# T5-bias attention followed by a leaky-ReLU feed-forward: the second feed-forward product as seven half-block products per 512-token tile, x in a ring of four batches, and a new order table

## The chip, the cores and the metric

The kernel runs on one core of one Trainium2 chip. The metric is device time in microseconds (us) of one execution, from outside the program; below it is given as the median of three executions. The profile is of one execution, and its span runs from the first to the last instruction of the core. The engines of the core are named as the profile names them: PE (matrix multiply; PEld is its loading of the stationary operand), DVE (vector), ACT (scalar and activation), POOL (here: memsets and the issue of loads) and SP (issue of transposing DMAs and of stores).

## What is computed

Eight batches of eight heads of attention (576 tokens, head size 64) with a relative-position bias, and then two products with a leaky ReLU between them, over all 4608 tokens:

```python
scores = scale * np.matmul(q, k.transpose(0, 1, 3, 2))          # 8, 8, 576, 576
bias = bias_table[bucket]
scores = scores + bias.transpose(2, 0, 1)[None, :, :, :]
attn = softmax(scores)
attn_out = np.matmul(attn, v)                                    # 8, 8, 576, 64
x = attn_out.transpose(0, 2, 1, 3).reshape(4608, 512)
h = x @ w_in                                                     # w_in 512 x 2048
g = np.maximum(0.01 * h, h)
out = g @ w_out                                                  # w_out 2048 x 512
```

Inputs and output are float32; the products run on bf16 operands with float32 sums.

## The kernel before

**Attention.** The work goes by items, one per batch and pair of heads: 32 items, `n = 4 * b + p`. For each item six units of scores go to PSUM (`score`, L424 to L432), ACT takes the exponential of each into the bf16 tile `at` (`expo`, L438, L440, L445), DVE multiplies the band near the diagonal by the exponentiated bias (`band`, L458), PE multiplies with v (`av` and `av_tail`, L478, L493), and DVE divides by the row sums into `opair` (`norm`, L505 and L506). `opair` is turned into `xT`, tokens along the free axis, in most items by a transposing DMA that SP issues (`x_dma`, L512), in the others by PE and a copy (`x_pe`, `x_copy`). q and k come in by POOL's loads, are copied into `pr` (L368), turned (by DMA into `tu`, or by PE) and copied into `qt` and `kt` (L399).

**Feed-forward.** The 4608 tokens are nine tiles of 512, `T = 0..8`. In a tile, the first product makes 16 blocks of 128 features: for each `f`, four matmuls of 512 columns into a PSUM bank (`ffn_in`, L536) and a leaky ReLU by ACT into the bf16 tile `gt` (`ffn_act`, L540). The second product takes the tile's four groups of 128 tokens one after the other: 16 matmuls of 512 columns each into one PSUM bank, with a block of `gt` as stationary operand and a block of `w_out_sb` as moving operand (`ffn_out`, L561), then a DVE copy into `y` (`ffn_y`, L566) and a 256 KB store by SP (`ffn_store`, L571). The last group of the last tile is cut by columns into 256, 128 and 128 (`ffn_end`, L547), each with a copy and a store of its own, so that little is left behind the last matmul. `gt` has two buffers, `y` four.

**PSUM** is eight banks: two double banks for scores (`S`), one bank for one head's attention output (`O`), and three banks (`M`) that everything else shares: the other head's output, the transposes and both feed-forward products.

**The order.** All engines run a program in a fixed order. The class `Plan` lists the work as tasks with costs, predecessors and PSUM slots and lays them out greedily; its tables `SHIFT`, `HOLD` and `SWAP` move single tasks in rank, hold them to a time or put them on another engine. What comes out is one order per engine, and each engine waits at an instruction until what that instruction needs is there. The feed-forward tasks fill PE between the attention steps, about 28 matmuls of 512 columns per item; what is left of them runs after the last item. The items are also paced by the first product (`PACE`, `LEAD` in `plan_pair`).

`w_out` is loaded as two halves by POOL (`load_w_out`, L342), behind the loads of the second batch. `xT` holds all 4608 tokens.

Of the kernel before, what the change touches and what calls it, by code (L numbers as in the profile page):

```python
# [36 lines left out]
class Plan:  # L37
# [5 lines left out]
        45: 10.5, 85: 76.5, 114: -31.5, 182: -25.5, 190: 10068.5, 237: -223, 253: 17.5, 327: 9898.5, 910:  # L43
        -9994.5, 916: -10001.5, 918: -9977.5, 920: -9885.5, 922: -9978.5, 928: -7, 940: -10006.5, 942: -22, 974:
        -10001.5, 978: -24.5,
# [7 lines left out]
    }  # L53

    SWAP = (19, 88, 91, 120, 184, 212,)
# [99 lines left out]
def kernel(  # L155
# [17 lines left out]
    P = 128  # L173
# [9 lines left out]
    BAND = 128  # L183

# [4 lines left out]
    pr_pool = ctx.enter_context(tc.tile_pool(name="pr", bufs=4))  # L189
    tu_pool = ctx.enter_context(tc.tile_pool(name="tu", bufs=4))  # L190
# [3 lines left out]
    y_pool = ctx.enter_context(tc.tile_pool(name="y", bufs=4))  # L194
# [65 lines left out]
    junk = per.tile([P, 512], BF16, name="junk")  # L260
# [248 lines left out]
    def x_dma(n):  # L509
        b, p = items[n]  # L510
        w = (NJ + 1) * P
        nc.sync.dma_start_transpose(  # L512
            out=xT[p][:, b * S : b * S + w].rearrange("p (i t) -> p i t", t=P),
            in_=opairs[n].rearrange("p i d -> p (i d)"),
        )
# [6 lines left out]
    def x_copy(n, t, lo=0, hi=S):  # L522
        b, p = items[n]
        mover(t)(out=xT[p][:, b * S + lo : b * S + hi], in_=outs.pop((n, "x", lo // P))[:, lo:hi])
# [4 lines left out]
    def ffn_in(T, f, cs=range(n_cc)):  # L529
        t0, w = tiles[T]  # L530
        if cs[0] == 0:
            if T not in gts:
                gts[T] = gt_pool.tile([P, n_fc, TT], BF16, name="gt", tag="gt")
            pms[T, f] = ps_m_pool.tile([P, TT], FP32, name="pm1", tag="m")
        for c in cs:
            nc.tensor.matmul(pms[T, f], lhsT=w_in_sb[:, c, f * P : (f + 1) * P], rhs=xT[c][:, t0 : t0 + w],  # L536
                             start=(c == 0), stop=(c == n_cc - 1))
# [4 lines left out]
    def ffn_end(T, ts, lo, hi):  # L542
        if lo == 0:
            ys[T, ts] = y_pool.tile([P, DM], FP32, name="y")
        ps = outs["end", lo] = ps_m_pool.tile([P, hi - lo], FP32, name="pm2", tag="m")
        for f in range(n_fc):
            nc.tensor.matmul(ps, lhsT=gts[T][:, f, ts * P : (ts + 1) * P], rhs=w_out_sb[:, f, lo:hi],  # L547
                             start=(f == 0), stop=(f == n_fc - 1))

    def ffn_end_y(T, ts, lo, hi, copy):  # L550
        copy(out=ys[T, ts][:, lo:hi], in_=outs["end", lo])

    def ffn_end_store(T, ts, lo, hi, eng):
        t0 = tiles[T][0] + ts * P
        eng.dma_start(out=out[t0 : t0 + P, lo:hi], in_=ys[T, ts][:, lo:hi])

    def ffn_out(T, ts, i):
        if i == 0:
            ys[T, ts] = ps_m_pool.tile([P, DM], FP32, name="pm2", tag="m")
        for f in range(4 * i, 4 * i + 4):  # L560
# [288 lines left out]
```

## Time and profile before

| | |
|---|---|
| time, median of three executions | 375.85 us (375.51 to 376.46) |
| span of the profiled execution | 373.5 us |
| median time less that span | 2.35 us |
| instructions in the profile | 8628 |
| granted PE clock | 1.000 |
| ACT, first product's leaky ReLU (L540) | 144 instructions, 605 ns each |
| POOL busy | 69.4 us (19% of the span) |
| bytes read and written | 36.70 MB and 9.44 MB |

An execution's own time is its span and what lies around it, before the first and after the last instruction of the core; the page gives the span, and the 2.35 us is the difference to the median of the three timed runs, all of which lie within 0.95 us of each other. A matmul's duration in the profile is longer than the time to the next matmul, since they are pipelined; the pace of a row of matmuls is found from its first start to its last start. The same holds, by less, for DVE.

### The profile page before, as it was taken

The numbers are of one execution on the slowest core, as the hardware profiler recorded it, in microseconds if no ns is written. First come the engines' busy times: TensorE is split into PE (matmuls) and PEld (weight loads), VectorE is DVE, ScalarE is ACT, GpSimd is POOL, SyncE is SP. The second block draws the span as 40 slices with busy tenths as digits, with TensorE's granted clock in tenths as the row PEclk, the third lists the DMA queues.
The fourth block names the chain that finished last, engine by engine and source line by source line (L and its number), as shares of the span: only waits on it lengthen the run. The fifth ranks groups of instructions, "written<-read, shape, count | busy, mean of one in ns | idle before, by whom it ended". The sixth has DMA issues, their size and how long they took to land.

```text
span 373.5 us, 8628 instructions
## 1 busy us (share of the span) xinstructions
PE 368.0 (99%) x3556; PEld 191.7 (51%) x3556; DVE 204.0 (55%) x550; ACT 243.7 (65%) x351; POOL 69.4 (19%) x107
## 2 busy tenths in 40 slices
PE   8999999999999999999999999999999999999996
PEld 5675555545555555545555555545555544444444
DVE  7997567786786557655755676555643311001021
ACT  5998987588756995697667866977678333333300
POOL 8856023340025003500350013000000000000000
PEclk9999999999999999999999999999999999999999
DMA  8999999999469907991899159201210101001012
GB/s 121 156 181 197 185 181 114 212 212 176 64 132 183 177 18 111 189 157 20 131 198 146 30 113 137 71 11 47 75 47 20 47 28 54 32 28 58 28 56 86
DMA packets 103735, 39.51 MB, mean 106 GB/s; under 512 B 83472, under 2 KB 98192, under 8 KB 103696
## 3 DMA queue, kind: packets, MB, share of 16 engines
q0 software_dynamic: 53424, 18.21, 46.2%
q1 hardware_dynamic: 49920, 20.39, 29.1%
q8 instruction: 28, 0.46, 0.5%
q10 hardware_dynamic: 352, 0.36, 0.3%
q14 instruction: 11, 0.09, 0.1%
HBM read 36.70 MB, written 9.44 MB: 124 GB/s over the span
## 4 chain that ended last, share of the span: by engine, by line
PE 95%; ACT 3%; DVE 1%; issue 1%; POOL 0%; POOLq 0%
PE pm L536 34%; PE pm L561 33%; PE ps_s L424 9%; PE ps_om L493 6%; PE ps_o L493 5%; ACT at L438 2%; PE ps_s L428 2%; PE ps_s L431 2%; PE pm L547 1%; PE ps_o L478 1%; PE ps_tx L520 1%; PE ps_t L382 0%; DVE hots L301 0%; PE ps_t L387 0%; PE ps_w L814 0%
## 5 line engine op out<-in xcount | busy, mean ns | idle before, releaser
L438 ACT ACTIVATE at<-ps_s 128x1024 bf16<-128x1024 f32 x124 | 120.4, 1028 | 32.8 <-PE ps_s L424 32.8
L536 PE MATMUL pm<-xT,w_in_sb 128*128 128x512 bf16 x576 | 140.8, 379 | 0.0
L561 PE MATMUL pm<-w_out_sb,gt 128*128 128x512 bf16 x560 | 135.5, 379 | 0.0
L540 ACT ACTIVATE gt<-pm 128x512 bf16<-128x512 f32 x144 | 84.8, 605 | 59.8 <-PE pm L536 58.8
L458 DVE TENSOR_TENSOR at<-at,hk 128x768 bf16<-128x768 bf16 (+4 forms) x156 | 69.5, 453 | 64.0 <-ACT at L438 47.1
L561 PEld LDWEIGHTS <-gt 128*128 128x128 bf16 x560 | 52.5, 98 | 64.7 <-issue 5.1
L536 PEld LDWEIGHTS <-w_in_sb 128*128 128x128 bf16 x576 | 52.2, 98 | 63.1 <-issue 6.4
L566 DVE COPY y<-pm 128x512 f32<-128x512 f32 x35 | 24.2, 691 | 70.6 <-PE pm L561 70.6
L236 POOL DMA_DIRECT2D vn<-in_v_dram x32 | 28.9, 911 | 141.3 <-PE ps_o L493 131.0
L493 PEld LDWEIGHTS <-at 128*128 128x128 bf16 x1240 | 41.2, 98 | 3.7 <-issue 0.7
L424 PE MATMUL ps_s<-qt,kt 64*128 64x512 bf16 x256 | 40.0, 381 | 0.3
L440 ACT ACTIVATE at<-ps_s 128x512 bf16<-128x512 f32 x31 | 18.7, 602 | 16.7 <-PE ps_s L428 16.6
L493 PE MATMUL ps_o<-vn,at 128*128 128x65 bf16 x640 | 25.5, 193 | 0.0
L493 PE MATMUL ps_om<-vn,at 128*128 128x65 bf16 x600 | 24.1, 195 | 0.0
L424 PEld LDWEIGHTS <-kt 64*128 64x128 bf16 x256 | 8.3, 94 | 24.7 <-issue 22.0
L445 ACT ACTIVATE at<-ps_s 128x576 bf16<-128x576 f32 x31 | 20.3, 654 | 0.8 <-PE ps_s L432 0.7
L506 DVE TENSOR_TENSOR opair<-ps_o,rcp 128x320 bf16<-128x320 f32 (+2 forms) x34 | 16.4, 482 | 1.2
L506 DVE TENSOR_TENSOR opair<-ps_om,rcp 128x320 bf16<-128x320 f32 (+2 forms) x32 | 15.4, 481 | 1.1
L399 DVE COPY kt<-tu 128x576 bf16<-128x576 bf16 x24 | 15.9, 663 | 0.0
L399 DVE COPY qt<-tu 128x576 bf16<-128x576 bf16 x23 | 15.0, 652 | 0.0
L505 DVE RECIPROCAL rcp<-ps_om 128x5 f32<-128x5 f32 (+2 forms) x32 | 6.1, 192 | 15.3 <-PE ps_om L493 15.3
L228 POOL DMA_DIRECT2D kn<-in_k_dram x17 | 12.1, 715 | 9.0 <-DMA w_in_sb<-in_moe_w_in_dram 3.9
(86 smaller groups left out, 238.3 us busy)
## 6 DMA issues: line engine op xcount, KB each, us to landing
out_dram<-y SPq DMA_DIRECT2D x35, 256.0 KB, 2.0
vn<-in_v_dram POOLq DMA_DIRECT2D x32, 128.0 KB, 6.9
qn<-in_q_dram POOLq DMA_DIRECT2D x14, 288.0 KB, 10.4
kn<-in_k_dram POOLq DMA_DIRECT2D x14, 288.0 KB, 10.8
w_in_sb<-in_moe_w_in_dram POOLq DMA_DIRECT2D x2, 1024.0 KB, 11.5
w_out_sb<-in_moe_w_out_dram POOLq DMA_DIRECT2D x2, 1024.0 KB, 19.6
qn<-in_q_dram POOLq DMA_DIRECT2D x4, 144.0 KB, 4.0
v<-in_v_dram POOLq DMA_DIRECT2D x16, 32.0 KB, 7.4
```

Source lines behind the costliest of these rows:

```text
L236: nc.gpsimd.dma_start(out=vn[i][:, c, :, 0:D], in_=v[b, :, c * P : (c + 1) * P, :].rearrange("h s d -> s h d"),)
L399: copy(out=t[:, 0:S].rearrange("p (r c) -> p r c", c=NC), in_=src)
L424: nc.tensor.matmul(ps[:, e, :], lhsT=kt[r, u * P : (u + 1) * P], rhs=qt[r, 0:512], start=True, stop=True)
L438: nc.scalar.activation(at[:, :, u, 0:512], ps, AF.Exp, scale=scale)
L445: nc.scalar.activation(at4[:, 0:S], ps.rearrange("p e i -> p (e i)")[:, 0:S], AF.Exp, scale=scale)
L458: nc.vector.tensor_tensor(out=o, in0=o, in1=m, op=ALU.mult)
L493: nc.tensor.matmul(ps[:, ic, :], lhsT=at[:, o : o + P], rhs=vn[i][:, c, 2 * p + e, :], start=whole and c == 0, stop=not whole and ic == NJ ...
L506: nc.vector.tensor_tensor(out=opairs[n][:, lo:hi, e * D : (e + 1) * D], in0=ps[:, lo:hi, 0:D], in1=rcp.to_broadcast([P, hi - lo, D]), op=A ...
L536: nc.tensor.matmul(pms[T, f], lhsT=w_in_sb[:, c, f * P : (f + 1) * P], rhs=xT[c][:, t0 : t0 + w], start=(c == 0), stop=(c == n_cc - 1))
L540: nc.scalar.activation(gts[T][:, f, :], pms.pop((T, f)), AF.Prelu, bias=0.0, scale=1.0, alpha=0.01)
L561: nc.tensor.matmul(ys[T, ts], lhsT=gts[T][:, f, ts * P : (ts + 1) * P], rhs=w_out_sb[:, f, :], start=(f == 0), stop=(f == n_fc - 1))
L566: nc.vector.tensor_copy(out=y, in_=ys[T, ts])
```

## The change

The second product of a tile is computed by Strassen's scheme in Winograd's form. `g` of the tile (512 tokens by 2048 features) is seen as two by two blocks: tokens 0 to 255 and 256 to 511, features in alternate groups of 128. `w_out` (2048 by 512) is seen as two by two blocks: the same alternate groups of 128 rows, and columns 0 to 255 and 256 to 511. Seven products of half-blocks replace eight.

- **PE.** Each product is two groups of 128 tokens by eight blocks of 128 features, that is 16 matmuls of 256 columns into one bank (`product`, L604 of the new kernel): 112 matmuls of 256 columns per tile in place of 64 of 512.
- **DVE, sums of g.** Four combinations of the blocks of `gt` (`mix_g`, L582), in two halves of the features: eight instructions of 128 x 1024 bf16 per tile. Three go to new single tiles `sums`, one is written over a block of `gt`.
- **DVE, sums of w_out.** Four combinations, once, in two halves (`mix_weights`, L568 to L571): eight instructions of 128 x 1024 bf16, behind the load of each half of `w_out`. One is written over a block of `w_out_sb`.
- **DVE, output.** In place of four copies of 128 x 512 per tile, each product is taken out of PSUM by one instruction that adds it to `y` (`combine`, L612 and L617): one copy and five sums of 512 elements, and one sum of 1024 for the product that two blocks share. Two of the nine copies go to ACT by `SWAP`.
- **Stores.** `y` is one buffer for a tile, and its two halves of 256 tokens are stored by two DMAs of 512 KB (`ffn_store`, L621). The cut of the last group is gone.
- **x.** `xT` holds four batches (2304 tokens) as a ring. A write of x of batch 4 or later waits for the first product of the tile that last reads what it overwrites (`free_x`). The tile that lies across the end of the ring (T = 4) runs each of its matmuls of the first product as two of 256 columns.
- **Buffers.** `pr` and `tu` have three buffers, not four.
- **Order.** `SHIFT`, `HOLD` and `SWAP` are new.

```diff
     SHIFT = {
-        45: 10.5, 85: 76.5, 114: -31.5, 182: -25.5, 190: 10068.5, 237: -223, 253: 17.5, 327: 9898.5, 910:
...
+        36: 486.5, 43: 362.5, 60: 11.5, 66: -54.5, 68: -313, 81: 1183.5, 119: -494.5, 126: -591.5, 150: 46, 176:
...
-    SWAP = (19, 88, 91, 120, 184, 212,)
+    SWAP = (62, 63, 88, 91, 117, 184, 212, 261, 269, 270, 952, 1141,)
...
+    NPR, NTU = 3, 3
...
-    xT = [per.tile([P, NT + P - SL], BF16, name=f"xT{p}") for p in range(n_pairs)]
+    RING = 4
+    RT = RING * S
+    xT = [per.tile([P, RT + P - SL], BF16, name=f"xT{p}") for p in range(n_pairs)]
...
+    NK = n_fc // 2
+    HT, HE = TT // 2, DM // 2
+    y = per.tile([P, 2, 2, 2, HE], FP32, name="y")
+    mix = per.tile([P, 3, NK, HE], BF16, name="mix")
+    sums = [per.tile([P, NK, HT], BF16, name=f"sum{i}") for i in range(3)]
...
+            for i, (o, x, n) in enumerate(spans):
+                nc.tensor.matmul(pms[T, f][:, o : o + n], lhsT=w_in_sb[:, c, f * P : (f + 1) * P], rhs=xT[c][:, x : x + n],
+                                 start=(c == 0 and i == 0), stop=(c == n_cc - 1 and i == len(spans) - 1))
...
-    def ffn_out(T, ts, i):
...
-        for f in range(4 * i, 4 * i + 4):
-            nc.tensor.matmul(ys[T, ts], lhsT=gts[T][:, f, ts * P : (ts + 1) * P], rhs=w_out_sb[:, f, :],
-                             start=(f == 0), stop=(f == n_fc - 1))
...
+    def mix_weights(lo, hi):
+
+        (b11, b12), (b21, b22) = [[w_blocks[:, lo:hi, h, g, :] for g in range(2)] for h in range(2)]
+        m2, m3, m4 = [mix[:, i, lo:hi, :] for i in range(3)]
+        nc.vector.tensor_tensor(out=m3, in0=b22, in1=b12, op=ALU.subtract)
+        nc.vector.tensor_tensor(out=b12, in0=b12, in1=b11, op=ALU.subtract)
+        nc.vector.tensor_tensor(out=m2, in0=b22, in1=b12, op=ALU.subtract)
+        nc.vector.tensor_tensor(out=m4, in0=b21, in1=m2, op=ALU.subtract)
...
+    def mix_g(T, k, lo, hi):
+
+        a11, a12, a21, a22 = [g_block(T, r, h, lo, hi) for r in range(2) for h in range(2)]
+        s1, s2, s4 = [t[:, lo:hi, :] for t in sums]
+        out_, x, y, op = ((s1, a21, a22, ALU.add), (s2, s1, a11, ALU.subtract),
+                         (a21, a11, a21, ALU.subtract), (s4, a12, s2, ALU.subtract))[k]
+        nc.vector.tensor_tensor(out=out_, in0=x, in1=y, op=op)
...
+    def product(T, k, ts):
+
+        if ts == 0:
+            pms[T, "p", k] = ps_m_pool.tile([P, 2, HE], FP32, name="pm2", tag="m")
+        ps = pms[T, "p", k]
+        of = factors(T, k)
+        for j in range(NK):
+            l, r = of(j)
+            nc.tensor.matmul(ps[:, ts, :], lhsT=l[:, ts * P : (ts + 1) * P], rhs=r,
+                             start=ts == 0 and j == 0, stop=ts == 1 and j == NK - 1)
+
+    def combine(T, k, copy=None):
+
+        c11, c12, c21, c22 = [y[:, r, :, g, :] for r in range(2) for g in range(2)]
+        ps = pms.pop((T, "p", k))
+        if k == 1:
+            copy(out=c22, in_=ps)
+            return
+        out_, x = {2: (c11, c22), 6: (c12, c22), 7: (c22, c12), 4: (c21, c22), 5: (y[:, :, :, 1, :],) * 2, 3: (c12, c12)}[k]
+        if k == 5:
+            ps = ps.unsqueeze(1).to_broadcast([P, 2, 2, HE])
+        nc.vector.tensor_tensor(out=out_, in0=ps, in1=x, op=ALU.add)
+
+    def ffn_store(T, r):
+        t0 = tiles[T][0] + r * HT
+        nc.sync.dma_start(out=out[t0 : t0 + HT, :].rearrange("(s p) e -> p s e", p=P),
+                          in_=y[:, r].rearrange("p s g e -> p s (g e)"))
...
+        free_x = [("in", ((b - RING + 1) * S - 1) // TT, n_fc - 1)] if b >= RING else []
...
+    ORDER = (1, 2, 6, 7, 4, 5, 3)
```

Where the order moved, at two places.

**The first tile's sums, DVE.** Before, at the place where the first output group of tile 0 is copied out of PSUM (`y<-pm`), DVE stands so (`at` bands, `kt`, `qt` and `pr` copies, `xT` copy):

```order
L458 TENSOR_TENSOR at_114<-at_114,hk 128x2x384
L399 COPY kt_110<-tu 128x576
L524 COPY xT_94<-ps_tx 128x576
L403 TENSOR_TENSOR kt_110<-kt_110,own 128x128
L403 TENSOR_TENSOR qt<-qt,own 128x128
L458 TENSOR_TENSOR at_114<-at_114,hk 128x2x320
L458 TENSOR_TENSOR at_1_116<-at_1_116,hk_100 128x192
L368 COPY pr<-qn_101 96x768
L368 COPY pr<-kn_103 96x768
L458 TENSOR_TENSOR at_113<-at_113,hk 128x2x256
L566 COPY y<-pm_1166 128x512
L458 TENSOR_TENSOR at_113<-at_113,hk 128x2x384
```

Now the second half of the sums of `w_out` (L568 to L571) and the second half of tile 0's sums of g (L582) stand between the bands of one item:

```order
L471 TENSOR_TENSOR at_116<-at_116,hk 128x2x384
L568 TENSOR_TENSOR mix<-w_out_sb 128x1024
L569 TENSOR_TENSOR w_out_sb<-w_out_sb 128x4x256
L570 TENSOR_TENSOR mix<-w_out_sb 128x1024
L571 TENSOR_TENSOR mix<-w_out_sb,mix 128x1024
L582 TENSOR_TENSOR sum_98<-gt 128x1024
L538 COPY xT_91<-ps_tx 128x576
L471 TENSOR_TENSOR at_1_118<-at_1_118,hk_102 128x192
L381 COPY pr<-qn_103 96x768
L381 COPY pr<-kn_105 96x768
```

Two rows of `pr` copies like the last two follow there, and then the item's last band (`at_116`, 128x2x320). The first band of that item stands ahead of the quoted rows, and between it and the last band DVE now has the four sums of `w_out` and one of g.

**The end, DVE and SP.** Before, the last rows of DVE are copies alone (the last group's two pieces are L551), and the last of SP are stores:

```order
L566 COPY y<-pm_5348 128x512
L566 COPY y<-pm_5368 128x512
L566 COPY y<-pm_5388 128x512
L551 COPY y<-pm_5409 128x256
L551 COPY y<-pm_5429 128x128
```

```order
L512 DMA_TRANSPOSE xT_94<-opair 128x5x128
L512 DMA_TRANSPOSE xT_95<-opair 128x5x128
L571 DMA out_dram<-y 128x512 x13
L555 DMA out_dram<-y 128x256
L555 DMA out_dram<-y 128x128
```

Now the last tile's sums of g stand between the sums into `y` (`pm_5830` and `pm_5854` are the last two products of tile 7, the five numbers above 5870 that stand here are tile 8's):

```order
L617 TENSOR_TENSOR y<-pm_5830,y 128x4x256
L582 TENSOR_TENSOR sum_98<-gt 128x1024 x2
L582 TENSOR_TENSOR sum_99<-sum_98,gt 128x1024
L617 TENSOR_TENSOR y<-pm_5854,y 128x2x256
...
L612 COPY y<-pm_5875 128x2x256
...
L617 TENSOR_TENSOR y<-pm_5896,y 128x2x256
...
L617 TENSOR_TENSOR y<-pm_5954,y 128x2x256
L617 TENSOR_TENSOR y<-pm_5972,y 128x4x256
L617 TENSOR_TENSOR y<-pm_5990,y 128x2x256
```

```order
L525 DMA_TRANSPOSE xT_93<-opair 128x5x128
L525 DMA_TRANSPOSE xT_90<-opair 128x5x128
L621 DMA out_dram<-y 128x2x512
L525 DMA_TRANSPOSE xT_91<-opair 128x5x128
L525 DMA_TRANSPOSE xT_92<-opair 128x5x128
L621 DMA out_dram<-y 128x2x512 x7
```

Behind the last matmul there now stands a sum of 512 elements and a store of 512 KB, where there stood ACT's copy of 128 elements and a store of 64 KB.

More of the change, by code (lines that the diff above doesn't have):

```diff
@@ L259 @@
     make_identity(nc, ident)
-    junk = per.tile([P, 512], BF16, name="junk")
+    junk = per.tile([P, 256], BF16, name="junk")
     nc.vector.memset(junk, 0.0)
@@ new lines, in plan_ffn @@
+        cb, last = {}, []
+        for n, k in enumerate(ORDER):
+            ps = prod[T, k] = []
+            for ts in range(2):
+                rank = 10000 + (T + 1) * 64 + (2 * n + ts) * 64 / 14 + 2
+                ps.append(add("PE", 0.876, acts + mixed + of.get(k, []) + last,
+                              lambda k=k, ts=ts: product(T, k, ts), rank, take=["M"] if ts == 0 else []))
+                last = ps[-1:]
+            before = [cb[i] for i in {1: (), 2: (1,), 6: (1,), 7: (6, 2), 4: (7,), 5: (7, 4), 3: (5,)}[k]]
+            if k == 2:
+                before = before + stored.get(T - 1, [])[1:]
+            if k == 1:
+                before = before + stored.get(T - 1, [])[:1]
+            cb[k] = add("DVE", 1.2 if k == 5 else 0.66, ps + before, lambda k=k: combine(T, k, mover(cb[1])), 0, give=["M"])
+            if k == 1:
+                cb[k]["other"] = ("ACT", 0.53)
+            if k == 5:
+                stored[T] = [add("SP", 0.1, [cb[5], cb[4]], lambda: ffn_store(T, 1), 10000, tail=2.5)]
@@ L806 @@
         plan_pair(n)
+    mixed = [add("DVE", 2.4, [L["w_out", h]], lambda h=h: mix_weights(h * NK // 2, (h + 1) * NK // 2), 10000)
+             for h in range(2)]
     for T in range(n_tt):
```

94 lines of the change are left out of this document (40 added, 54 removed), and 15 rows, old and new, of tables (HOLD, SHIFT).

## The prediction

> **What bounds the kernel now.** I read the page first: shares of the engines, the slices, and the chain of work that ended last.
>
> ```profile
> span 373.5 us, 8628 instructions
> PE 368.0 (99%) x3556; PEld 191.7 (51%) x3556; DVE 204.0 (55%) x550; ACT 243.7 (65%) x351; POOL 69.4 (19%) x107
> PEclk9999999999999999999999999999999999999999
> PE 95%; ACT 3%; DVE 1%; issue 1%; POOL 0%; POOLq 0%
> PE pm L536 34%; PE pm L561 33%; PE ps_s L424 9%; PE ps_om L493 6%; PE ps_o L493 5%; ACT at L438 2%; PE ps_s L428 2%; PE ps_s L431 2%; PE pm L547 1%; PE ps_o L478 1%; PE ps_tx L520 1%; PE ps_t L382 0%; DVE hots L301 0%; PE ps_t L387 0%; PE ps_w L814 0%
> ```
>
> PE is busy for 99% of the span at full clock and makes 95% of the chain; the second product (L561) alone is a third of it. A busy PE need not be at its peak, so I looked at the pace of matmuls that follow each other in the timeline, with the mean durations from the groups of instructions by shape.
>
> ```profile
> 361.75 5.34 PE L561 MATMUL pm<-w_out_sb,gt 128*128 128x512 bf16 x24
> 366.93 1.25 PE L547 MATMUL pm<-w_out_sb,gt 128*128 128x256 bf16 x10
> 366.93 3.70 PE L547 MATMUL pm<-w_out_sb,gt 128*128 128x256 bf16 x48
> L561 PE MATMUL pm<-w_out_sb,gt 128*128 128x512 bf16 x560 | 135.5, 379 | 0.0
> L547 PE MATMUL pm<-w_out_sb,gt 128*128 128x256 bf16 x16 | 1.9, 272 | 0.0
> ```
>
> In the first, second and third row the columns are start, length from first start to last end, and count. Start to start, 512 columns take (5.34 - 0.379) / 23 = 0.2157 us, and 256 columns (1.25 - 0.272) / 9 = 0.109 us, almost exactly half. The third row is the whole last token group of today: 3.70 us. So PE's time is proportional to columns at this size, and PE really is the bound: columns removed are time removed, wherever PE keeps finding its operands ready.
>
> **The products, on the path.** A tile takes 64 x 0.2157 = 13.80 us before and 112 x 0.109 = 12.21 us after: 1.59 us less. Eight tiles give 12.7 us. The ninth takes 48 x 0.2157 + 3.70 = 14.05 us before, so 1.84 us less. Sum **-14.5 us**. The tile across the ring's end runs 128 matmuls of 256 in place of 64 of 512 in its first product: 128 x 0.109 - 64 x 0.2157 = **+0.15 us**. The rest of PE's work is unchanged in kind and count, but for two more warming matmuls at the start.
>
> The weight loads beside these matmuls double in density. They are a row of their own:
>
> ```profile
> L561 PEld LDWEIGHTS <-gt 128*128 128x128 bf16 x560 | 52.5, 98 | 64.7 <-issue 5.1
> 108.04 0.79 PE L493 MATMUL ps_om<-vn,at 128*128 128x65 bf16 x20
> ```
>
> A load lasts 98 ns, under the 109 ns of a 256-column matmul, and in the second row twenty matmuls of 65 columns, each with a load, start within 0.79 us, so at most 0.04 us apart. Loads do not set the pace at 256 columns; I count nothing for them.
>
> [...]
>
> **The end, on the path.** Today a small copy by ACT and a small store follow the last matmul.
>
> ```profile
> 370.66 0.27 ACT L551 COPY y<-pm 128x128 f32<-128x128 f32 x1 [14.16 <-PE pm L547]
> 370.96 0.38 ACTq L555 DMA_DIRECT2D out_dram<-y  x1
> out_dram<-y SPq DMA_DIRECT2D x35, 256.0 KB, 2.0
> out_dram<-y ACTq DMA_DIRECT2D x1, 64.0 KB, 1.7
> L566 DVE COPY y<-pm 128x512 f32<-128x512 f32 x35 | 24.2, 691 | 70.6 <-PE pm L561 70.6
> ```
>
> The last matmul ends at 366.93 + 3.70 = 370.63 and the span at 373.5: 2.87 us. After the change a 512-element sum (0.69 us as the copy in the last row, 0.42 more than the 0.27) and a 512 KB store follow. Its landing isn't in the trace: 1.7 us as for 64 KB is the least, and doubling the 2.0 us of the 256 KB store is the most, 4.0. From 64 to 256 KB cost 0.3 us, so I take 2.8, nearer the 2.0: 1.1 more. Sum **+1.5 us**, bounds +0.4 to +2.7.
>
> **DVE, which now has to keep up.** The new instructions' forms aren't in the trace, so I take them from the nearest rows.
>
> ```profile
> L458 DVE TENSOR_TENSOR at<-at,hk 128x768 bf16<-128x768 bf16 x62 | 34.0, 553 | 12.6 <-ACT at L438 12.4
> L458 DVE TENSOR_TENSOR at<-at,hk 128x512 bf16<-128x512 bf16 x32 | 13.5, 423 | 34.7 <-ACT at L438 34.7
> L506 DVE TENSOR_TENSOR opair<-ps_o,rcp 128x320 bf16<-128x320 f32 x32 | 15.7, 492 | 1.1
> 40.00:280.00 240.00, 240.00 (x2427) 123.02 (x2425) 154.06 (x409) 178.09 (x250) 42.15 (x55) 1.00 0.91 120
> 60.00:80.00 20.00, 20.00 (x217) 10.46 (x216) 16.71 (x42) 11.95 (x16) 9.29 (x13) 1.00 1.47 175
> ```
>
> Two bf16 operands in SBUF cost (553 - 423) / 256 = 0.51 ns per element, so a sum of 1024 takes 0.68 us. With float32 from PSUM it is (691 - 492) / 192 = 1.04 ns, so 1024 elements take 1.22 us and 512 take 0.69. A tile gets 8 x 0.68 + 6 x 0.69 + 1.22 = 10.8 us, less the four copies of 2.8: **8.1 us more DVE per tile**, and 8 x 0.68 = 5.5 us once for `w_out`. The last two rows are busy time by stage (after the window's length PE, PEld, DVE, ACT, POOL): in the 240 us where attention and feed-forward are mixed, DVE was busy 154 us, 64%. By the order, about six tiles' second products lie there: 154 + 6 x 8.1 + 5.5 = 208 us, 87%. The fullest 20 us of before had 16.71, 84%, with PE busy throughout. So on average PE covers DVE, with little to spare; ACT's work is the same but for two copies.
>
> What counts then are lumps. In the timeline the same place of two successive items starts so:
>
> ```profile
> 104.65 2.76 PE L561 MATMUL pm<-w_out_sb,gt 128*128 128x512 bf16 x12
> 113.83 0.39 PE L561 MATMUL pm<-w_out_sb,gt 128*128 128x512 bf16 x1
> ```
>
> An item is 9.18 us. The thickest lump is tile 0: eight sums of `w_out` and eight of g, 16 x 0.68 = 10.9 us, within about two items, so DVE's 64% of 18.4, 11.8 us, becomes 22.7: 4.3 too much. Behind these sums in DVE's order stand the item's last band, which `av` waits for, and the normalization, on which x hangs. PE has about half an item, 4.6 us, of other work between a score and its `av`; that absorbs most. The wait for `w_out` in DVE's queue is the other thing there:
>
> ```profile
> L342 POOL DMA_DIRECT2D w_out_sb<-in_moe_w_out_dram x2: 876/884/891, 29.0 to 30.8; - x2
> DMA to landing us min/median/max: 17.3/19.6/22.0
> ```
>
> The second half lands by 30.8 + 22.0 = 52.8 us, and DVE comes to it about an item after the first half's sums, near 54; what is later is paid by the bands behind it. Bounds of this lump: 0, if the cover holds, to 4.3 + 1; I take **+1.5**. Later tiles bring eight sums and no `w_out`: 5.4 us in the same two items, so 11.8 + 5.4 + 3.8 for combines, 21.0 against 18.4 at the worst, and idle DVE time around them (the L566 row above: 70.6 us of waiting for L561 alone). Bounds 0 to 2.6 for each of five; I take **+0.5** in all, near the lower end since the sums need only be done before the third product of a tile, 3.5 us of PE after the first begins.
>
> At the end, tile 8's sums (5.4 us) stand among tile 7's and 8's combines (5.4 us per tile): 10.8 us in the 12.2 us of a tile's products; sums of g wait until tile 7's last products have read the old ones. The first product that needs them is the third, 3 x 1.74 us after product 5 of tile 7 plus 0.86 for the last matmuls of L536: 6.1 us, and they take 1.2 + 4 x 0.68 + 0.69 = 4.6. I count nothing; without that cover it is 1 to 2 us.
>
> Counted at nothing as well: three buffers for `pr` and `tu` (a turning DMA has two items, 18 us, of lead), the ring's waits (x of batch 7 needs the first product of tile 4, which stands some four items earlier in the order), and stores, now 18 in place of 38 and one buffer, which the last tile's first combine needs back 4.4 us after tile 7's product 5, some 4.0 us after which the store lands (1.2 for the sum, 2.8).
>
> **Sum.** -14.5 + 0.15 + 1.5 + 1.5 + 0.5 = -10.85. On the profiled execution: 373.5 - 10.85 = 362.65 us of span, with the 2.35 us between span and median 365.0 us. The profile agrees with the timed runs as far as their 0.95 us of spread goes.
>
> **The rivals.**
>
> *DVE sets the pace of the mixed stage.* If the 84% of its fullest window are all that its in-order queue can be filled, 208 us need 248: 8 us more than the 240, in place of the 2.0 above, so **371 us**. For it: the bands wait for ACT and now stand behind sums. Against: PE was fully busy at 84%.
>
> *Slower: the sums run at one element per cycle.* If `gt` cut into strided blocks costs the 1.04 ns per element of the PSUM rows, a sum takes 1.22 us, and the 56 of the mixed stage need 30 us more: 238 of 240. At a fill of 90% that stage lasts 264 us: 24 more, **387 us**. It decides from about 1.0 us per sum on. Against: the bands, also cut in runs and one operand reversed, take 0.51 ns.
>
> *PE doesn't gain.* If 256-column matmuls run at 0.1232 us or more (13.80 / 112) when operands change between `gt`, sums and mixes, nothing is gained and end and lumps are paid: **379 us**. Ten in a row at 0.109 speak against it.
>
> *More is gained.* Lumps hidden, store as quick as one of 256 KB, and an order that waits 2 us less in the first 30 us: 375.85 - 14.35 + 0.7 - 2 = **360 us**.
>
> **How the numbers follow.** Forecast, 361.5 to 368: 0.68. Better: 0.08. DVE's pace, 368 to 374.7: 0.14. Gain eaten up by it exactly, within 0.3% (what a measurement of this kernel can tell from no change): 0.03. Slower: 0.05 by slow sums, 0.02 by PE's pace. So faster 0.90, same 0.03, slower 0.07. The range for 8 in 10 is 360.5 to 371.5: it takes in half of the better and half of DVE's case.
>
> **What would show it.** Products: 1008 matmuls of 256 columns, ten of them in about 1.25 us, and some 110 us in the second product in place of 124. DVE: sums near 0.68 us, the big combine near 1.22, DVE busy near 280 us in all. Lumps: PE's idle time or stretched runs between 45 and 70 us, released by DVE. End: some 4.4 us from the last matmul to the end of the span. The forecast is wrong if sums take over 1 us, if the mixed stage lasts longer than before with DVE ahead of PE in the waits, or if PE's pace at 256 columns isn't half of that at 512.

## The result, and the profile after

| | before | after |
|---|---|---|
| time, median of 11 executions (lowest to highest) | 376.46 us (375.51 to 376.99) | 370.59 us (368.09 to 374.37) |
| ratio after/before, 95% interval | | 0.9833 (0.9803 to 0.9863) |
| profiled execution, its own time | | 368.75 us |
| its span, mean granted PE clock | 373.5 us, 1.000 | 367.0 us, 0.998 |

The ratio leaves out the executions most disturbed by a low clock. The gain is 5.9 us at the median where 11 were forecast; and the kernel, steady within 1.5 us before, now varies by 6. Its executions have mean granted clocks from 0.999 (368.1 us) to 0.989 (373.0 to 374.4 us).

The page of the changed kernel, the rows that answer to those of before:

```profile
span 367.0 us, 9617 instructions
PE 355.8 (97%) x4022; PEld 239.7 (65%) x4022; DVE 266.8 (73%) x650; ACT 246.5 (67%) x356; POOL 71.8 (20%) x107
PE 87%; DVE 5%; ACT 3%; DMA 3%; issue 1%; ACTq 0%
PE pm L556 32%; PE pm L604 28%; PE ps_s L437 8%; PE ps_om L506 5%; PE ps_o L506 5%; DMA tu<-pr 3%; ACT at L451 2%; PE ps_s L441 2%; PE ps_s L444 2%; PE ps_w L879 2%; DVE at L471 1%; PE ps_o L491 1%; DVE sum L582 1%; PE ps_tx L533 1%; DVE opair L519 0%
```

PE is still the bound, but its share of the span fell from 99% to 97%. In the chain DVE grew from 1% to 5%, and 3% DMA are new, all of one kind, the DMA that turns `pr` into `tu`. The new instructions' durations, from the groups by shape (busy us, mean ns of one, idle before):

```profile
L582 DVE TENSOR_TENSOR sum<-gt 128x1024 bf16<-128x1024 bf16 x18 | 12.3, 688 | 11.1 <-ACT gt L560 11.0
L617 DVE TENSOR_TENSOR y<-pm,y 128x512 f32<-128x512 f32 x45 | 30.9, 686 | 12.8 <-PE pm L604 11.3 <-DMA out_dram<-y 1.1
L617 DVE TENSOR_TENSOR y<-pm,y 128x1024 f32<-128x1024 f32 x9 | 11.0, 1223 | 8.0 <-PE pm L604 8.0
```

0.69, 0.69 and 1.22 us, as estimated from the nearest rows of before. The last of the chain's longest rows gives the pace of the products:

```profile
348.11 13.99 PE pm L604 x128
```

13.99 / 128 = 0.109 us per 256-column matmul. The product's price was right. What was not right stands between 40 and 80 us. PE's busy time there is the number behind the window's length; the first row is of before, the other two of after:

```profile
40.00:60.00 20.00, 20.00 (x211) 10.64 (x209) 12.14 (x33) 17.51 (x25) 4.54 (x7) 1.00 1.70 171
40.00:60.00 20.00, 18.92 (x211) 10.87 (x211) 17.99 (x41) 18.39 (x27) 5.45 (x8) 1.00 1.72 176
60.00:80.00 20.00, 17.52 (x234) 13.15 (x233) 15.66 (x41) 11.19 (x16) 5.25 (x5) 1.00 1.04 118
```

Before the change both windows had 20.00 (the row from 60 to 80 us stands in the prediction). PE's waits between 40 and 100 us (us in total, times, longest), where before has none at all:

```profile
PE ps_om L491 <- DVE y L617: 1.7, 1, 1.7
PE ps_om L506 <- DVE at L471: 0.8, 1, 0.8
PE ps_s L437 <- ACT at L453: 0.7, 1, 0.7
PE ps_s L437 <- ACT at L451: 0.2, 1, 0.2
```

The two longest are one event. The chain from 66 to 74 us shows it from its cause on (start, length, what):

```profile
60.68 9.75 DMA tu<-pr
...
70.46 0.62 DVE pr L381 x2
71.08 0.57 DVE at L471 x2
71.66 0.60 DVE y L617
```

and DVE's timeline shows what waited:

```profile
70.46 0.36 DVE L381 COPY pr<-qn 96x768 bf16<-96x768 bf16 x1 [4.20 <-DMA tu<-pr]
```

DVE stood idle for 4.20 us at a `pr` copy, that of item 11. With three `pr` buffers it takes the one that item 9 used, and item 9's turning DMA, issued at 60.68 us, landed 9.75 us later. Before the change item 9's DMA took 8.3 us, not much less, but with four buffers no `pr` copy waited for it. Nobody needed item 11's copy yet: what is made of it is copied out of `tu` at 86.32 us. But behind it in DVE's order stood two bands, a sum into `y` and then more bands. The sum frees the PSUM bank that the next `av_tail` opens, the bands are `av`'s operand:

```profile
70.41 0.19 PE L491 MATMUL ps_o<-v,at 64*128 64x65 bf16 x1
72.31 0.19 PE L491 MATMUL ps_om<-v,at 64*128 64x65 bf16 x1 [1.71 <-DVE y L617]
...
73.38 0.79 PE L506 MATMUL ps_om<-vn,at 128*128 128x65 bf16 x20 [0.76 <-DVE at L471]
```

From start to start PE loses 72.31 - 70.41 = 1.90 us, and 0.95 more ahead of the last row: **2.85 us**. At the end of the span:

```profile
360.83 1.26 PE L604 MATMUL pm<-w_out_sb,sum 128*128 128x256 bf16 x10
361.62 1.59 SPq L621 DMA_DIRECT2D out_dram<-y  x2
362.12 0.69 DVE L617 TENSOR_TENSOR y<-pm,y 128x512 f32<-128x512 f32 x1 [0.52 <-PE pm L604]
```

and the landing of the last two stores, from the DMA view (count, KB each, median us):

```profile
out_dram<-y SPq DMA_DIRECT2D x2, 512.0 KB, 2.9
```

The last matmul ends at 360.83 + 1.26 = 362.09 us, the span at 367.0: 4.9 us, where 4.4 was forecast.

### The profile page after: what moved, and what is told of

Its sections match the earlier page's. It is cut to its first block, busy times and chain, and to the rows that moved or that the text cites. A ratio compares the mean times of both kernels' runs of the same rounds, so it can differ in the third digit from the quotient of the medians.

```text
span 367.0 us, 9617 instructions
## 1 busy us (share of the span) xinstructions
PE 355.8 (97%) x4022; PEld 239.7 (65%) x4022; DVE 266.8 (73%) x650; ACT 246.5 (67%) x356; POOL 71.8 (20%) x107
## 4 chain that ended last, share of the span: by engine, by line
PE 87%; DVE 5%; ACT 3%; DMA 3%; issue 1%; ACTq 0%
PE pm L556 32%; PE pm L604 28%; PE ps_s L437 8%; PE ps_om L506 5%; PE ps_o L506 5%; DMA tu<-pr 3%; ACT at L451 2%; PE ps_s L441 2%; PE ps_s L444 2%; PE ps_w L879 2%; DVE at L471 1%; PE ps_o L491 1%; DVE sum L582 1%; PE ps_tx L533 1%; DVE opair L519 0%
## 5 line engine op out<-in xcount | busy, mean ns | idle before, releaser
L556 PE MATMUL pm<-xT,w_in_sb 128*128 128x512 bf16 (+1 forms) x640 | 134.1, 358 | 0.0
L556 PEld LDWEIGHTS <-w_in_sb 128*128 128x128 bf16 x640 | 59.1, 98 | 57.1 <-issue 5.1
L471 DVE TENSOR_TENSOR at<-at,hk 128x768 bf16<-128x768 bf16 (+4 forms) x156 | 67.1, 448 | 30.6 <-ACT at L451 22.6
L604 PEld LDWEIGHTS <-gt 128*128 128x128 bf16 x576 | 54.6, 98 | 10.8 <-issue 3.6
L617 DVE TENSOR_TENSOR y<-pm,y 128x512 f32<-128x512 f32 (+1 forms) x54 | 41.9, 775 | 20.8 <-PE pm L604 19.3
L604 PEld LDWEIGHTS <-sum 128*128 128x128 bf16 x432 | 41.3, 98 | 9.6 <-issue 2.5
L604 PE MATMUL pm<-w_out_sb,sum 128*128 128x256 bf16 x288 | 35.4, 273 | 0.0
L604 PE MATMUL pm<-mix,gt 128*128 128x256 bf16 x288 | 34.8, 273 | 0.0
L604 PE MATMUL pm<-w_out_sb,gt 128*128 128x256 bf16 x288 | 33.9, 273 | 0.0
L582 DVE TENSOR_TENSOR sum<-gt 128x1024 bf16<-128x1024 bf16 x18 | 12.3, 688 | 11.1 <-ACT gt L560 11.0
L604 PE MATMUL pm<-mix,sum 128*128 128x256 bf16 x144 | 17.7, 273 | 0.0
```

What stands on the lines that cost most here:

```text
L471: nc.vector.tensor_tensor(out=o, in0=o, in1=m, op=ALU.mult)
L556: nc.tensor.matmul(pms[T, f][:, o : o + n], lhsT=w_in_sb[:, c, f * P : (f + 1) * P], rhs=xT[c][:, x : x + n], start=(c == 0 and i == 0), s ...
L604: nc.tensor.matmul(ps[:, ts, :], lhsT=l[:, ts * P : (ts + 1) * P], rhs=r, start=ts == 0 and j == 0, stop=ts == 1 and j == NK - 1)
L617: nc.vector.tensor_tensor(out=out_, in0=ps, in1=x, op=ALU.add)
```

## The experiments

Theory A: PE sets the pace throughout, and what is missing against the forecast is that one wait and the end. Rival B: DVE's new load holds PE back through the whole mixed stage. On the varying clock, theory X: PE's gap lowers it; theory Y: the denser stream of matmuls and weight loads does. Each ratio is to the kernel before, run on the same chip. Runs 1 to 4, 5 to 8, 9 to 11 and 12 had a chip each, so between these groups ratios are compared, not times.

**1. The changed kernel again**, as the base for the three runs beside it on the same chip.

> The changed kernel unaltered, as the base for the runs beside it. Both theories of the path: span 366.3 to 367.5 us where the granted clock is 0.998 or above, with DVE idle about 4.2 us ahead of the pr copy of item 11 near 66 us and PE idle 2.8 us between 70.4 and 73.4 us. Clock: its earlier runs had mean granted clocks of 0.989 to 0.999 and times of 368.1 to 374.4 us, and the same spread of about 6 us is expected again; if it is gone, the spread belonged to the chip or the hour and not to the kernel.

Measured: 372.18 us (369.21 to 375.97, six executions), ratio 0.9877 (0.9847 to 0.9906), clocks 0.986 to 0.995; profiled span 367.4 us at 0.994. The spread was there again, so it belongs to the kernel. This time the profile caught a low clock, seen in windows of 5 us, and then of 1 us (the third number from the right):

```profile
65.00:70.00 5.00, 4.90 (x43) 3.29 (x42) 1.33 (x5) 2.55 (x4) 0.00 (x0) 1.00 1.35 149
70.00:75.00 5.00, 3.15 (x56) 2.66 (x56) 4.93 (x15) 1.64 (x2) 1.06 (x2) 0.81 0.40 72
75.00:80.00 5.00, 4.95 (x38) 3.22 (x38) 4.49 (x8) 2.15 (x4) 5.00 (x7) 0.85 1.48 95
80.00:85.00 5.00, 4.95 (x76) 3.63 (x77) 4.68 (x16) 4.34 (x6) 2.05 (x3) 1.00 1.45 152
```

```profile
74.00:75.00 1.00, 1.00 (x7) 0.73 (x5) 0.96 (x4) 0.00 (x0) 1.00 (x2) 0.50 0.07 16
75.00:76.00 1.00, 1.00 (x7) 0.69 (x6) 0.68 (x2) 0.00 (x0) 1.00 (x2) 0.50 0.39 25
```

PE waited 1.2 us before 71.1 and 0.8 us before 72.2 in this execution; the clock falls to half just behind that, and is back by 80 us.

**2. Item 9's `pr` in memory of its own.** Every engine's order is as before.

```diff
-            prs[n] = pr_pool.tile([RQ, 2, NC, 2 * D], BF16, name="pr")
+            if n == 9:
+                o = ATW + SL + S + SL
+                prs[n] = extra[0:RQ, o : o + 4 * NC * D].rearrange("r (j c d) -> r j c d", j=2, c=NC)
+            else:
+                prs[n] = pr_pool.tile([RQ, 2, NC, 2 * D], BF16, name="pr")
```

> Only the pr buffer of item 9 is placed in memory of its own (the dead end of the early scratch tile), so that the pr copies of item 11 no longer wait for the turning DMA of item 9; every engine's order is as before. Theory A (the loss beside the forecast is this one stall, PE sets the pace elsewhere): DVE's 4.2 us of idle time at 66 us goes, PE's gaps of 1.9 and 0.95 us at 70.4 and 72.4 us go, span 367.0 - 2.85 = 364.2 us (363.5 to 364.8), time about 366. Rival B (DVE's load in the first tile holds PE back, the wait only sits where DVE would have been late anyway): the gaps come back within 20 us at another DVE wait, span 366.3 to 367.5. Clock: theory X (the 3 us gap in PE's work lowers the granted clock later) expects 0.998 or above in every run and a spread of times under 1 us; theory Y (the denser stream of weight loads and matmuls lowers it) expects 0.989 to 0.999 and 5 us of spread, as in the kernel it is made from.

Measured: 366.06 us (365.54 to 371.30), ratio 0.9737 (0.9715 to 0.9760), span 363.8 us. The windows, and then the longest waits of PE from 40 to 100 us, of this kernel:

```profile
40.00:60.00 20.00, 18.63 (x210) 11.17 (x212) 18.06 (x41) 18.23 (x27) 5.68 (x8) 1.00 1.65 177
60.00:80.00 20.00, 19.95 (x271) 15.05 (x270) 18.82 (x47) 13.50 (x19) 8.27 (x10) 1.00 1.40 148
```

```profile
PE ps_s L441 <- ACT at L457: 0.7, 1, 0.7
PE ps_s L441 <- ACT at L455: 0.2, 1, 0.2
```

PE is full from 60 to 80 us again, with DVE at 18.82 of 20: A, not B. The span fell by 367.4 - 363.8 = 3.6 us. The 2.85 us of the first profile are not to be compared with that: in run 1's own profile PE's gap was 1.38 + 0.95 = 2.3 us from start to start, and the low clock cost 1.7 us more. On the clock X is borne out in part: four of six executions at 0.998 or above, but two at 0.992, and the times spread by 5.8 us where X expected under 1.

**3. The end split**: the last product in two banks, each half summed and stored by itself.

```diff
...
+    def end_sum(T, ts):
+        o = y[:, 0, ts, 1, :]
+        nc.vector.tensor_tensor(out=o, in0=pms[T, "p", 3, ts][:, ts, :], in1=o, op=ALU.add)
...
```

> The last product of the last tile is written as two halves in two PSUM banks, and each half is combined and stored by itself (128x256 on DVE, then a store of 256 KB). Theory A (the tail after the last matmul is a serial chain of combine, store issue and landing): combine 0.69 to about 0.40 us, and a 256 KB store lands sooner than the 512 KB one of 3.4 us, so the 4.90 us behind the last matmul become 3.3 to 4.0: span 367.0 - 0.9 to -1.6 = 365.4 to 366.1 us at a clock of 0.998. Rival (the landing is a fixed cost whatever the size, or the two stores delay one another): tail 4.5 to 4.9, span 366.5 to 367. No change before 355 us in either.

Measured: 368.82 us (368.24 to 370.20), ratio 0.9807 (0.9787 to 0.9827), span 367.6 us. The timeline of its end, and the landing of its last stores:

```profile
360.78 2.02 PE L605 MATMUL pm<-w_out_sb,sum 128*128 128x256 bf16 x17
362.41 0.84 DVE L611 TENSOR_TENSOR y<-pm,y 128x256 f32<-128x256 f32 x2
362.87 1.23 SPq L615 DMA_DIRECT2D out_dram<-y  x2
```

```profile
out_dram<-y SPq DMA_DIRECT2D x2, 256.0 KB, 3.0
```

The last matmul ends at 362.80 and the span 4.8 us later, against 4.9: the rival held. 256 KB landed in 3.0 us, 512 KB in 2.9; halving the store bought nothing. The bytes in flight at the end are the same in both (1.05 MB from 355 us on), and the first half's sum did not come early: DVE was at the sum of product 5 until 362.3 us. So a smaller last store by itself was not tried. The ratio below that of run 1 goes with the clock (0.994 to 0.998 here): at the same 0.994 the two spans are 367.6 and 367.4.

**4. Both together.**

> The item 9 buffer of its own and the split end together. Theory A: the two savings add, span 367.0 - 2.85 - 1.2 = 363.0 us (362.3 to 363.7), time about 364.8 at a clock of 0.998, which is faster than both kernels. Rival B (the stall covers time that is lost anyway): 365.4 to 366.1, as with the split end alone.

Measured: 366.51 us (365.49 to 367.18), ratio 0.9738 (0.9719 to 0.9757), span 364.2. As run 2 alone; the sum that A expected is missing its part from the end.

**5. PE's gap filled with junk matmuls.**

```diff
...
+        if n == 2 * n_pairs - 1:
+            for _ in range(24):
+                nc.tensor.matmul(outs[n, 0].rearrange("p c d -> p (c d)")[:, 0:256], lhsT=junk[:, 0:P], rhs=junk[:, 0:256],
+                                 start=True, stop=True)
...
```

> The changed kernel with its stall left in, but PE's 3 us gap near 70 us filled by 24 junk matmuls of 256 columns (24 x 0.109 = 2.6 us) that PE would otherwise idle through; DVE's idle time of 4 us at 66 us stays. The span of a run at full clock is as in the kernel it is made from, 366.3 to 367.5 us. Theory X (PE's gap is what makes the granted clock fall afterwards): the clock between 70 and 80 us, 0.81 and 0.85 in the profile of the unaltered kernel on this chip, becomes 1.00, the mean clock 0.998 or above in nearly every run, and the times lie within about 1.5 us, median 367.5 to 369 where the unaltered kernel had 372.2. Theory Y (the denser stream of loads and matmuls lowers the clock): mean clocks of 0.986 to 0.995 and a median of 371 to 373 as before.

Measured: 369.86 us (369.21 to 373.09), ratio 0.9838 (0.9801 to 0.9875). Four of six executions had clocks of 0.996 to 1.000 and spans of 367.4 to 368.3 us, where the unaltered kernel had four such clocks in 17 (none of run 1's six, four of the result's eleven); the profiled one, at 0.993, shows what can still happen. From its chain, and then its windows:

```profile
60.58 12.33 DMA tu<-pr
```

```profile
70.00:75.00 5.00, 3.67 (x39) 2.64 (x38) 2.07 (x8) 1.94 (x2) 0.00 (x0) 1.00 0.98 135
75.00:80.00 5.00, 4.23 (x60) 3.73 (x54) 4.34 (x11) 0.00 (x0) 1.62 (x2) 0.66 0.32 59
```

The DMA landed after 12.33 us this time, so the gap came behind the junk matmuls instead of under them, and the clock fell behind the gap; the span is 371.0 us. So the wait's length differs between executions with one DMA's landing. X is supported, not proven: the gap was moved, not filled, and the median lies above the 367.5 to 369 that X expected.

**6. Before, with each 512-column matmul of the second product run as two of 256.**

> The kernel before the change, with each 512-column matmul of its second product run as two of 256 columns, the same block of g loaded for each: 560 more matmuls and loads, nothing else. If 256 columns take 0.109 us at 512's 0.2157 us (the term of the forecast): 560 x (2 x 0.109 - 0.2157) = +1.3 us, 376.2 + 1.3 = 377.5 us, and no more than +2 us. Rival (256-column matmuls cost 0.123 us or more): +17 us, 393 us. Clock: theory X (gaps lower it, and this kernel has none) 0.999 to 1.000 in all runs and a spread of times under 2 us; theory Y (density lowers it) 0.986 to 0.997 and a spread of 4 us or more.

Measured: 377.40 us (376.80 to 378.46, twelve executions), ratio 1.0021 (1.0007 to 1.0035), clocks 0.999 to 1.000 in all. 0.8 us for 560 more matmuls and loads, a little under the 1.3 expected: the pace of 256 columns is what the forecast took. PEld is as busy here as after the change (246.5 and 239.7 us), and no clock fell. Y falls.

**7 and 8. Run 2 without the sums of w_out; and without those and the sums of g.** The products take plain blocks in their place. These kernels leave out the sums alone; the matmuls are as many.

```diff
...
-                                lambda k=k, lo=lo, hi=hi: mix_g(T, k, lo, hi), 5 * k)
+                                lambda: None, 5 * k)
...
-    mixed = [add("DVE", 2.4, [L["w_out", h]], lambda h=h: mix_weights(h * NK // 2, (h + 1) * NK // 2), 10000)
+    mixed = [add("DVE", 2.4, [L["w_out", h]], lambda: None, 10000)
...
```

> Made from the kernel with item 9's pr apart (span 363.8): the eight sums of w_out are left out, products 4, 6 and 7 take plain blocks of w_out instead, same count of matmuls. Theory A (the lump of 16 sums in tile 0 costs what PE lost between 40 and 60 us, 2.1 us more than before the change, and nothing later): span 361.7 to 362.9, the gain all before 62 us. Rival B (DVE's load holds PE back through the whole mixed stage): the eight sums are only 5.5 us of some 208, so the gain is under 0.5 us. Rival C (the loss between 40 and 60 us comes from ACT or from the new order, not from DVE's sums): no change, 363.5 to 364.1.

> As the run without the sums of w_out, and the 72 sums of g are left out as well (all seven products take plain blocks of g and of w_out; same matmuls). Theory A: beside the 40 to 60 us stage nothing is gained but some tenths in the later tiles: span 361.0 to 362.2. Rival B (DVE's load paces the mixed stage): 49 us less DVE work, PE's loss against its own pace between 80 and 280 us falls by 2 us or more, span under 360.5. Rival C: 363.3 to 364.1.

Measured: 366.27 us (365.21 to 367.61), ratio 0.9723 (0.9694 to 0.9751); and 366.09 us (365.15 to 366.79), ratio 0.9715 (0.9688 to 0.9741). Run 2 had 0.9737. With 80 sums of 0.69 us, 55 us of DVE work, gone, nothing is gained that can be told from no change: rival C (the loss comes from ACT or the new order) stands, and B falls. The traces say the same of B directly: from 76 to 280 us in the changed kernel, and from 64 to 280 us in run 2, PE has no wait at all. The windows of the run without any sums:

```profile
40.00:60.00 20.00, 18.67 (x205) 10.39 (x207) 12.04 (x34) 18.61 (x28) 5.67 (x8) 1.00 1.56 180
```

PE's loss from 40 to 60 us is the same with DVE at 12.04 as with DVE at 18.06. The profiled execution of run 7 was 2 us longer than run 2's (365.8 us of span), by a wait of 2.2 us for `xT`, whose turning DMA landed after 11.4 us. That of run 8 had 365.0; the others of both runs lie between 363.4 and 364.7.

**9. The loads of batch 3 later.** POOL issues four loads of q and k between 56 and 60 us, just ahead of item 9's turning DMA. Here a one-column memset on DVE and one on POOL hold them until the `pr` copies of item 10.

```diff
...
+        if b == 3 and held is not None:
+            held.append((b, h0, h1, js))
+            return
...
+        nc.vector.memset(extra[:, 7000:7001], 0.0)
+        nc.gpsimd.memset(extra[:, 7000:7001], 0.0)
+        for args in loads:
+            load_qk(*args)
...
```

> The changed kernel with its three pr buffers, but the four loads of q and k for batch 3 (288 KB each, issued on POOL between 56 and 60 us) are held until the pr copies of item 10, about 63.5 us, by a one-column memset on DVE and one on POOL. Theory Q (the turning DMA of item 9, issued at about 60.5 us, lands late, after 9.0 to 12.3 us, because its packets share the DMA engines with these loads): it lands in 3.5 to 6 us, DVE's wait ahead of item 11's pr copy falls from 3.5 to 6.7 us to under 1, span 363.5 to 364.8 us, clock 1.00 between 70 and 80 us, spread of times under 2 us. Rival R (a turning DMA is slow there by itself, or by the loads issued earlier): landing 9 us or more, span 366.3 to 371 as without the change. A cost that either could have: batch 3's first pr copy (73 us) waits for its loads by up to 2 us.

Measured: 366.93 us (365.98 to 368.68), ratio 0.9757 (0.9735 to 0.9780), span 364.3 us at 0.999. The landing of the one turning DMA issued between 59.5 and 62 us (count, median us), in the changed kernel and in this one:

```profile
tu<-pr SPq DMA_TRANSPOSE x1, 9.8
```

```profile
tu<-pr SPq DMA_TRANSPOSE x1, 4.1
```

Theory Q: the loads beside it make it late. Run 11, on the same chip and with the loads in their old place, has 9.4 us. Three buffers suffice where it lands in 4 us. The times spread by 2.7 us, not by under 2 as expected. The fall from 9.8 to 4.1 us came with the loads moved; in what way they delay the DMA, no run here shows.

**10. The loads later and item 9's `pr` apart.**

> The loads held as in the run above and item 9's pr in memory of its own as well. Theory Q: span 363.3 to 364.3 us, as with the buffer alone at its best (363.8), but without its slower runs (two of six had clocks of 0.992 and 366 to 369.5 us of span): all times within 1.5 us. Rival R: spread as with the buffer alone, or a new wait of DVE for batch 3's loads near 73 us that costs 1 to 2 us in every run.

Measured: 366.08 us (365.33 to 366.82), ratio 0.9730 (0.9710 to 0.9751), clock 0.999 in all four executions, span 364.9. The same DMA with `pr` apart (`extra`), in run 2 and here:

```profile
tu<-extra SPq DMA_TRANSPOSE x1, 9.6
```

```profile
tu<-extra SPq DMA_TRANSPOSE x1, 3.3
```

Run 2's executions at a clock of 0.992 did not show in four, which is few; it is no faster than run 2's best.

**11. Run 2 with item 7's `qt` copy on DVE in place of ACT.**

```diff
...
-                 lambda: take_turned(n, 0, mover(cq)), feed, give=give)
+                 lambda: take_turned(n, 0, nc.vector.tensor_copy if n == 2 * n_pairs - 1 else mover(cq)), feed, give=give)
...
```

> Made from the kernel with item 9's pr apart: the one copy of qt of item 7 (1.27 us on ACT at 52.3 us) is done by DVE (0.64 us), nothing else moves. Theory C (between 49 and 59 us ACT is the bound: its work is unbroken for 10.2 us and the scores at 56 us wait for it 0.85 + 0.54 us): PE's two gaps of 1.4 us near 56 us shrink to 0.1 to 0.5, the excess of the 40 to 60 us stage falls by about 1 us, span 363.8 - 1.0 = 362.8 us (362.4 to 363.2). Rival (these gaps are set by something else, such as DVE's copies behind the sums, where DVE gets 0.64 us more): no change or up to 0.6 us slower.

Measured: 366.80 us (365.59 to 366.97), ratio 0.9747 (0.9729 to 0.9764), span 363.8: no change. The waits say why:

```profile
PE ps_t L399 <- DVE pr L385: 0.8, 1, 0.8
PE ps_s L441 <- ACT at L457: 0.3, 1, 0.3
```

The wait for ACT fell from 0.7 to 0.3 us, and at 59.5 us one of 0.8 appeared for a `pr` copy that stands behind the sums of w_out on DVE. So the wait for DVE stands right behind that for ACT.

**12. Run 8 with ACT lightened too**: the `qt` copy and two blocks of g of tile 0 (as plain copies, without the leaky ReLU) on DVE.

```diff
...
+        if (T, f) in ((0, 14), (0, 15)):
+            nc.vector.tensor_copy(out=gts[T][:, f, :], in_=pms.pop((T, f)))
+            return
...
```

> Made from the run without any sums (its DVE is idle for 4 of the 10 us from 50 to 60): ACT is lightened as well. The qt copy of item 7 (1.2 us on ACT) goes to DVE, and so do the last two blocks of g of tile 0, as plain copies without the leaky ReLU (2 x 0.6 us on ACT). Theory C (in the 40 to 60 us stage both DVE's sums and ACT's unbroken row of work hold PE, so that taking away either alone shows nothing): PE's gaps of 0.82 and 0.53 us at 57 us go, no gap of 0.9 us near 59.5 us as in the run with only the copy moved; PE idle or late time from 46 to 62 us falls by 1.2 to 1.6 us, span 1.0 to 1.5 us below that of the run without sums at its best (363.4), so 361.9 to 362.6 in the faster runs. Rival (the gaps come from the order on PE itself, for want of other matmuls until the first product can start at 57.8 us, and move elsewhere): span 363 to 365 as before, gaps of the same sum at other places.

Measured: 366.24 us (365.12 to 371.08), ratio 0.9738 (0.9715 to 0.9761). The wait for ACT at L457 fell to 0.2 us and none for `pr` came, as theory C has it, but 0.5 us is a third of what it expected and does not show in the time: spans of 363.3 to 365.4 us in all but the profiled execution. That one had span 369.3 us; its longest wait from 40 to 100 us and the clock behind it:

```profile
PE pm L560 <- DMA xT<-opair: 3.7, 1, 3.7
```

```profile
70.00:80.00 10.00, 6.31 (x70) 4.09 (x67) 7.84 (x18) 3.59 (x7) 7.53 (x8) 0.84 1.75 138
80.00:90.00 10.00, 9.95 (x96) 5.93 (x96) 5.55 (x16) 6.47 (x10) 1.34 (x2) 0.82 1.74 154
```

Here the late DMA is the one that turns x, which took 14.4 us. In runs 7 and 12 it is what PE waits for once `pr` no longer waits.

## Why the prediction was right, and where not

The time fell inside the range for 8 in 10, and the direction and the bound were right, but 365.0 was 5.6 us too low. That 370.59 still lies under the upper bound of 371.5 is luck in part. It is not in the forecast's own 361.5 to 368; it is where the prediction put DVE's pace (371 us, chance 0.14), and DVE's pace is not what happened.

In spans: 362.65 forecast, 367.0 measured, 4.35 us apart. 2.85 is the wait for item 9's buffer and 0.5 the end. The remaining 1.0 is not one wait. An estimate, made by counting each start of a matmul in both traces against the median step between its two shapes, puts 2.0 us more loss than before on 40 to 62 us, where the lump had 1.5, and 0.7 more on the first 20 us, a term that the sum did not have. Run 2, without the wait, measured 363.8.

The median adds 1.84 us over the profiled execution; the median execution had a clock of 0.994, the profiled one 0.998. Against this, the 2.35 us between span and median were 0.6 too many. Only 1.75 us lie outside the span of the profiled execution after, and as much before: one of the timed executions of before beside run 9 took 375.26 us with a span of 373.5. The other 0.6 was the distance between a quick profiled execution and the median.

- **Products, -14.5 us: right.** 0.109 us per matmul in the changed kernel, and +0.2% in run 6 for the same work in 256 columns without the saving. Weight loads, counted at nothing, cost nothing that showed.
- **"Three buffers for `pr` and `tu` (a turning DMA has two items, 18 us, of lead)", counted at nothing: the step that failed.** The lead was counted to the turned data's use. But a buffer must be free when the next copy into it comes up in DVE's order, and here item 11's copy comes up at 66.3 us, 5.6 us after item 9's DMA was issued. The copy waits early for something that nobody needs yet, and in-order DVE makes everybody behind it wait, here for 4.20 us. With the buffer given back, 3.6 us of span and 1.4% of the time came back against run 1. Run 9, which leaves the three buffers and makes the DMA land sooner, gets nearly as far. A place further back in DVE's order for item 11's copy, with three buffers, was not tried.
- **The end, +1.5: mis-sized, 2.0.** The landing was 2.9 us against 2.8 taken; the other 0.4 lies outside the sum and the landing, which these rows do not split. Halving the last store gained nothing (run 3).
- **The lump of tile 0, +1.5 by DVE: about the size, not the cause.** PE lost 1.08 us of busy time from 40 to 60 us (2.0 by the count of starts), but runs 7 and 8 show no gain without the sums. The wait named is ACT's (0.7 and 0.2 us). Before, the first output matmul of tile 0 starts at 49.41 us, now at 58.28. The plan lets a product start behind all 16 blocks of g and the sums of `w_out` (`acts + mixed`), where an output group started behind 12 blocks. In run 8, which has no sums, it starts no earlier, at 59.15 by its chain:

```profile
49.41 1.89 PE L561 MATMUL pm<-w_out_sb,gt 128*128 128x512 bf16 x8
```

```profile
58.28 1.92 PE L604 MATMUL pm<-w_out_sb,gt 128*128 128x256 bf16 x16
```

  Until then the first product is all that PE has to fill in between the attention steps, and each of its blocks costs ACT 0.6 us. That this crowds ACT is argued from these rows; no run changed the plan. Run 11 shows that DVE's row of work stands right behind ACT as the next wait, and run 12, with both lightened, gives PE 0.5 us back and gains nothing in time. What all of the stage's loss is made of stays open.
- **Later lumps, +0.5: none that run 8 shows.** Leaving all sums out gained nothing that shows (0.9715 against run 2's 0.9737). DVE was busy for 194.7 us from 40 to 280 us where 208 were forecast, and in run 2 it filled 18.82 of 20 us with PE at 19.95, so 84% is not all that it can be filled. DVE's load did not set the pace, and that rival is out.
- **The slower rival, sums at the 1.04 ns per element of the PSUM rows: out**, 0.69 us against its 1.22. **PE doesn't gain: out.**

Of the versions tried, run 2 beats both kernels: 366.06 us, 2.6% below before, and run 10 does as well with less spread.

## What to carry to other kernels

When a change takes a buffer away, look up in the engine's order where the next write into that buffer stands, and compare that moment with the landing of the slowest reader in flight; the lead of the data is not the slack of the buffer. On an in-order engine, a wait for something not urgent costs what stands behind it: here DVE's 4.20 us cost PE 2.85. And where a kernel's times spread, look for a wait whose end is a DMA's landing among bulk loads: here moving four loads by 7 to 8 us did nearly as much as another buffer (0.9757 against 0.9737).

## What was not expected of the hardware

**A turning DMA's landing varies widely beside loads.** Item 9's took 9.75, 9.22, 9.04 and 12.33 us in four profiled executions of kernels that wait for it (the result, runs 1, 3 and 5), 8.6 to 13.5 us in six that don't (runs 2, 4, 7, 8, 11 and 12), and 4.1 and 3.3 us with the four 288 KB loads held back.

**A gap in PE's work can be paid twice, in steps of 1.7 us.** Where the clock fell, the loss is the shortfall times the window: run 1, (0.19 + 0.15) x 5 = 1.7 us; run 3, (0.22 + 0.12) x 5 = 1.7; run 5, 0.34 x 5 = 1.7; run 12, (0.16 + 0.18) x 10 = 3.4. One step is 1.7 / 367 = 0.005 of the mean clock, and the executions of the changed kernel lie mostly near 0.999, 0.994 and 0.989. It followed PE waits of 1.8 to 2.1 us in total (runs 3, 1 and 5) and, as two steps, one of 3.7 us (run 12), but not the 2.5 us of the first profile after the change, nor the 2.2 us of run 7; kernels profiled without such a wait (before, runs 2, 4, 6, 8, 9, 10 and 11) show none between 40 and 100 us. That a gap is needed fits these traces; what decides whether the clock falls stays open. In run 1's profile the granted clock was 0.50 from 74 to 76 us, behind waits of 1.2 and 0.8 us with nine short matmuls between them.
